# A linear-attention and spectral-mix kernel: where the channel products stand, and which engine takes the absorbs out of PSUM

## The chip, the cores and the metric

The kernel runs on one core of a Trainium2 chip. The metric is the device time of one execution in microseconds (us). Beside the times there is one profiled execution with its trace. The engines are called PE (matrix products), DVE (vector), ACT (scalar and activation), POOL (general, and here the queue that loads the weights) and SP (stores). In the stage of interest, PSUM is used as four buffers of one bank named `pt` and two buffers of two banks named `pp`.

## The reference

```python
def phi(x):                                   # q and k, per head, 576 x 64
    proj = x @ w_phi                          # 128 features
    proj = proj - max(abs(proj), axis=-1)
    return concat([exp(proj), exp(-proj)])
kv, z = phi(k).T @ v, phi(k).sum(axis=seq)
x = (phi(q) @ kv) / (phi(q) @ z + 1e-6)       # as (8, 576, 512)

X = rfft(x, axis=seq)                         # 64 of 289 modes are kept
Y[:, m] = X[:, m] @ (w_r[m] + 1j * w_i[m])    # 512 x 512 for each mode
u = x + irfft(Y, n=576)
out = u + relu(u @ w_ch)
```

Two of 8 batches make a batch pair `bp`. The weights `w_r`, `w_i` are 64 MB each in float32 and are all read once.

## The kernel before, in words

**Attention stage.** A loop of 19 steps over 16 units (channel group `g` of four, batch pair `bp` of four) fills `xs` (x in bfloat16, with positions in 9 chunks of 128 rows per batch pair) and `XT` (its kept modes). Weight tiles of 1 MB, one for each channel group, octet of modes `o` and part `i` (real, imaginary), arrive through POOL's queue in nine buffers `wt`, and each is used by a *mix*: eight matmuls `pt<-wt,XT` into one bank `py` per octet. Mixes for the first groups run inside the attention stage.

**The stage around the change.** The last 22 mixes come after it: what is left of the third channel group, octets 0 to 5 of the last one, then octet 6 and octet 7 with four mixes each (two groups, two parts). Each weight tile is waited for in that order. When an octet is complete, its result y goes from PSUM to `yst`, is transposed on PE to `yT`, is multiplied with `w_ch` into z (`zst`), and both are parked in `yacc` by DVE transposes (`park`). `lay(bp)` copies what is parked for one batch pair into `yall` and `zall`: two DVE transposes, and the same after octet 6 again for pair 0.

Between the mixes stands a list `todo` of small pieces, taken one by one by `fill(n)`; `n` is worked out from what is left of the list and of the mixes (`left`). It holds two kinds:

- *Channel products*, 36 chunks (`Channels`, lines 715 to 738). `turn` transposes a chunk of x on PE into a bank and copies it to `xT` by DVE; `product` multiplies it with `w_ch` into a bank, which ACT copies to `xw`. The first pieces also advance `inverse_tables`, which makes the tables CI, CL and CM, mostly on DVE, with three Sin activations on ACT.
- *Absorbs*, 36 chunks (`Absorb`, lines 750 to 802). `sum_p` makes the back transform of y for a chunk in p, and DVE adds it to x in place. `sum_q` does the same for z in q, with xw added by an identity matmul, and ACT copies q to xw. Of the first 28 absorbs in the list, every second is *aside*: it leaves out the identity matmul, ACT copies q to a spare tile `rl`, and POOL adds it to xw. Even places of the list take p and q as the two halves of one `pp` buffer, odd places as two `pt` buffers.

Before, three of the chunks (`ab[K:]`, K = 33) are treated apart: their products stay in PSUM (`hold` of `Channels`), and `only_x` and `only_w` finish them when `yall` and `zall` are there. The list is products 0 to 32, the three holds, three `only_x`, three `only_w`, 33 whole absorbs. Line 996 leaves two products for the place behind octet 5, and line 1001 spreads what remains over the last mixes:

```python
        if left > 8:
            n = -(-max(len(todo) - A - 2, 0) // (left - 8))
        elif left == 8:
            n = 2
        else:
            n = math.ceil(len(todo) / max(left - 0.6, 0.4)) if left else 0
```

The chunks that the tail needs first (`direct`, six of pair 0) are absorbed last, since they need octet 6 too. **The tail** begins with the last mix. Before it stand some identity matmuls ("bases"); behind it octet 7 is finished, and 18 pairs of chunks are summed, passed through relu and stored, in an order written out by hand (`plan`). All engines keep program order (`InOrder`); a wait of one instruction holds everything behind it on its engine.

Of the kernel before, what the change touches and what calls it, by code (L numbers as in the profile page):

```python
# [10 lines left out]
F32 = mybir.dt.float32  # L11
# [3 lines left out]
ALU = mybir.AluOpType  # L15
# [28 lines left out]
def kernel(  # L44
# [449 lines left out]
    def chunk(bp, n):  # L494
        if n < 8:
            return xs[:, :, bp, 2 * n:2 * n + 2, :].rearrange("p g h d -> p g (h d)")
        return xs[:, :, bp, 16:18, :].rearrange("p g h d -> p g (h d)")
# [100 lines left out]
    def bank(shape=(128, DMODEL), dt=F32):  # L598
        return pst.tile(list(shape), dt, name="pt", tag="pt")

    def banks(dt=F32):
        return pst2.tile([128, 2, DMODEL * (1 if dt == F32 else 2)], dt, name="pp", tag="pp")
# [112 lines left out]
    class Channels:  # L715
# [4 lines left out]
        def turn(self):  # L720
            x = chunk(self.bp, self.n)
            pt = bank([128, 4, 128], BF16)
            for g in range(NG):
                pe.transpose(pt[:, g, :], x[:, g, :], ident_b)
            self.xT = pb.tile([128, 4, 128], BF16, name="xT")
            dve.tensor_copy(self.xT, pt)

        def product(self):
            pf = bank()
# [2 lines left out]
                          start=(g == 0), stop=(g == 3))  # L732
            act.copy(xw[:, self.bp, self.n, :], pf)

        def hold(self, pf):
            for g in range(NG):
                pe.matmul(pf, lhsT=self.xT[:, g, :], rhs=wchb[:, g, :],
                          start=(g == 0), stop=False)

    def back(p, c, bp, table, src, r, stop=True, start=False):  # L740

        if c < 8:
            pe.matmul(p, lhsT=table[r, c % 4, :], rhs=src[r, 2 * bp + c // 4, :],
                      start=start or src is yall, stop=stop)
        else:
            for i in range(2):
                pe.matmul(p[64 * i:64 * i + 64, :], lhsT=table[r, 4, 0:64],
                          rhs=src[r, 2 * bp + i, :], start=start or src is yall, stop=stop)

    class Absorb:  # L750

        def __init__(self, bp, n):
            self.bp, self.n = bp, n
            self.early = (bp, n) in direct
            self.rows = slice(0, 128)
            self.aside = False

        def sum_p(self, p):
            self.p = p
            back(p, self.n, self.bp, CI, yall, self.rows)  # L760

        def sum_q(self, q):
            self.q = q
            if not self.aside:
                pe.matmul(q, lhsT=ident_b, rhs=xw[:, self.bp, self.n, :], start=True, stop=False)
            back(q, self.n, self.bp, CI, zall, self.rows, start=self.aside)

        def keep_x(self):
            x = chunk(self.bp, self.n)
            dve.tensor_tensor(out=x, in0=self.p.rearrange("p (g e) -> p g e", g=4),  # L770
                              in1=x, op=ALU.add)

        def keep_w(self):
            w = xw[:, self.bp, self.n, :]
            if self.aside:
                if not spare:
                    t = pb.tile([128, 2, DMODEL], F32, name="rl")
                    spare.extend((t[:, 1], t[:, 0]))
                t = spare.pop()
                act.copy(t, self.q)  # L780
                pool.tensor_tensor(out=w, in0=t, in1=w, op=ALU.add)
            else:
                act.copy(w, self.q)

        def only_x(self):
            self.sum_p(bank())
            self.keep_x()

        def only_w(self):
            back(self.q, self.n, self.bp, CI, zall, self.rows)  # L790
            self.keep_w()

        def all(self):
            if full.index(self) % 2:
                p, q = bank(), bank()
            else:
                t = banks()
                p, q = t[:, 0], t[:, 1]
            self.sum_p(p)
            self.sum_q(q)  # L800
            self.keep_x()
            self.keep_w()

    chunks = [(bp, n) for bp in range(NP) for n in range(9)]
    ch = [Channels(*c) for c in chunks]
    ab = [Absorb(*c) for c in chunks]
    K = len(ch) - 3
    full = sorted(ab[:K], key=lambda c: c.early)
    spare = []
    for c in full[0:28:2]:  # L810
        c.aside = True

    tables = inverse_tables()

    def hold(i):
        next(tables, None)
        if i + 1 < len(ch):
            ch[i + 1].turn()
        if i < K:
            ch[i].product()  # L820
            return
        if i == K:
            t = banks()
            ab[i].q, ab[i + 1].q = t[:, 0], t[:, 1]
        elif i == K + 2:
            ab[i].q = bank()
        ch[i].hold(ab[i].q)

    todo = [ch[0].turn] + [lambda i=i: hold(i) for i in range(len(ch))]
    todo += [c.only_x for c in ab[K:]] + [c.only_w for c in ab[K:]] + [c.all for c in full[:-2] + full[:-3:-1]]  # L830
    A = 3 * 3 + K

    def fill(n):
        for _ in range(n):
# [31 lines left out]
    class Pair:  # L866
# [32 lines left out]
        def sums(self, side, a):  # L899
            (bp, n), at, z = self.items[a], self.at(side, a), self.z(side)  # L900
            start = not self.based(side)
            if self.straight:
                pe.matmul(at, lhsT=CM[n // 4][:, n % 4], rhs=zst if z else yst, start=start,
                          stop=True)
            else:
                r = 64 * a + 32 * z
                back(at, n, bp, CL, yl, slice(r, r + 32), True, start)
            self.left[side] -= 1

        def keep(self, a):  # L910
# [63 lines left out]
        assert mark is None  # L974

    H = DMODEL // 2
    while mixq:
        key = mixq.pop(0)
        g, o, i = key[0], key[1] // 2, key[1] % 2
# [14 lines left out]
        if left == 6:  # L994
            yl = pw.tile([128, B_, DMODEL], BF16, name="yl", tag="wt")
        if left > 8:
            n = -(-max(len(todo) - A - 2, 0) // (left - 8))
        elif left == 8:
            n = 2
        else:  # L1000
            n = math.ceil(len(todo) / max(left - 0.6, 0.4)) if left else 0
        if g == NG - 1 and i == 1:
            end = left == 0
            py = pys.pop(o)
            yst = pb.tile([128, DMODEL], BF16, name="yst")
            pt = [bank([128, 2, 128], BF16) for h in range(2)]
            yT = [pb.tile([128, 2, 128], BF16, name=f"yT{h}") for h in range(2)]
            if end:
                dve.tensor_copy(yst[:, 0:H], py[:, 0:H])
                act.copy(yst[:, H:], py[:, H:])  # L1010
            else:
                for h in range(2):
                    dve.tensor_tensor(out=yst[:, H * h:H * h + H], in0=py[:, H * h:H * h + H],
                                      in1=(yacc[:, o] if o < 6 else late[:, o - 6])[:, H * h:H * h + H], op=ALU.add)
            put(yst, o, 0, (0, 2))
            if o < 5:
                fill(min(n, 1))
            for h in range(2):
                if end:
                    until(f"T{h}")  # L1020
                for dc in range(2):
                    pe.transpose(pt[h][:, dc, :],
                                 yst[:, H * h + 128 * dc:H * h + 128 * dc + 128], ident_b)
                if h or end:
                    dve.tensor_copy(yT[h], pt[h])
                else:
                    act.copy(yT[h], pt[h])
            if o < 7:
                park(yst, o, 0)
            if o < 5:  # L1030
                fill(min(n - 1, 1))
            cut = (slice(0, 384), slice(384, DMODEL))
            pz, marks = [], ["z0a", "z0b", "z1"]
            zst = pb.tile([128, DMODEL], BF16, name="zst")
            for e in range(2):
                for h in range(2):
                    if end and marks:
                        until(marks.pop(0))
                    if h == 0:
                        pz.append(bank([128, cut[e].stop - cut[e].start]))  # L1040
                    for dc in range(2):
                        pe.matmul(
                            pz[e], lhsT=yT[h][:, dc, :], rhs=wchb[:, 2 * h + dc, cut[e]],
                            start=(h == dc == 0), stop=(h == dc == 1))
                if e:
                    dve.tensor_copy(zst[:, cut[1]], pz[1])
                else:
                    act.copy(zst[:, cut[0]], pz[0])
            put(zst, o, 1, (1, 3))
            if o < 7:  # L1050
                park(zst, o, 1)
            if o == 5:
                lay(3)
                lay(0)
            elif o == 6:
                assert all(f.__self__.early or f.__self__.bp for f in todo)
                lay(0)
            fill(max(n - 2, 0) if o < 5 else n)
        else:
            fill(n)  # L1060
    assert not todo
# [33 lines left out]
```

## Time and profile before

| | |
|---|---|
| times of three runs | 436.51, 436.1, 438.81 us; median 436.51 |
| the profiled execution | 436.92 us |
| its span, first to last instruction | 435.1 us |
| mean granted PE clock | 0.911 of full speed |
| busy: PE, DVE, ACT, POOL | 75%, 70%, 67%, 28% of the span |
| octet 5's last mix | 356.29 us from the span's start |
| last weight tile issued | 365.83 us |
| last mix | 401.12 us |

How to read it: the page gives busy shares over the whole span, though stages have different limits; its slices are the span in 40 equal parts, one digit each for the busy tenths. A timeline row has start, length, engine, operation, result and operands, count, and the idle time before it with what ended it. All instructions carry one line number, that of the helper that records them, so tiles tell them apart: `xT`, `xw`, `xs`, `rl`, `wt`, `yall`, `zall`.

### The profile page before, as it was taken

To read this page: it belongs to the slowest core of one execution; us is meant where nothing else is said; L and a number is where in the kernel's file an instruction comes from. 1 tells how busy PE (TensorE), PEld (TensorE's weight loads), DVE (VectorE), ACT (ScalarE), POOL (GpSimd) and SP (SyncE) were. 2 spreads that over 40 slices of the span, in tenths; PEclk is the share of its full clock that TensorE was granted. 3 is DMA by queue.
4 is the path that set the end of the run, shared out by engine and by line. 5 is a ranking of instruction groups with operands and counts; after the bars stand their busy time and mean duration, and the time that the engine had idled before them with its cause. 6 is when DMAs were issued, how large, how long until landed. Compare 5 with 4: busy or idle time off the path is not lost.

```text
span 435.1 us, 10067 instructions
## 1 busy us (share of the span) xinstructions
PE 328.3 (75%) x4205; PEld 196.1 (45%) x4205; DVE 306.7 (70%) x608; ACT 291.5 (67%) x473; POOL 120.2 (28%) x158
## 2 busy tenths in 40 slices
PE   1567668678697686886976866946899867979993
PEld 1345546456465454554654644622345433333320
DVE  6768676765676677887678879728854445997794
ACT  3788696776977978887778779613444331656871
POOL 6232132123211212222222221221111100574790
PEclk9779897789988989997789999968999998999997
DMA  9999999999999999999999999999999999993797
GB/s 215 209 211 211 238 211 238 235 214 241 235 211 239 216 232 239 237 212 238 223 226 235 213 256 216 211 212 213 212 212 212 212 212 212 212 214 80 231 392 295
DMA packets 49879, 97.71 MB, mean 225 GB/s; under 512 B 2314, under 2 KB 11530, under 8 KB 49834
## 3 DMA queue, kind: packets, MB, share of 16 engines
q0 software_dynamic: 45136, 85.40, 100.4%
q1 hardware_dynamic: 4538, 11.60, 7.1%
q8 instruction: 33, 0.54, 0.5%
q10 hardware_dynamic: 160, 0.07, 0.1%
q14 instruction: 12, 0.10, 0.1%
HBM read 163.64 MB, written 9.44 MB: 398 GB/s over the span
## 4 chain that ended last, share of the span: by engine, by line
PE 34%; ACT 26%; DMA 17%; DVE 17%; issue 4%; POOL 1%; ACTq 0%; DVEq 0%; POOLq 0%
PE one L37 13%; ACT AQ L37 11%; ACT AB L37 9%; PE pt L37 8%; DMA wt<-in_moe_w_i_dram 8%; DMA wt<-in_moe_w_r_dram 8%; PE two L37 8%; DVE m L37 5%; PE pp L37 4%; ACT XT L37 3%; ACT qT L37 2%; DVE xs L37 2%; DVE mk L37 2%; DVE of L37 1%; DVE xw L37 1%
## 5 line engine op out<-in xcount | busy, mean ns | idle before, releaser
L37 ACT ACTIVATE AQ<-two 128x1024 bf16<-128x1024 f32 x64 | 80.4, 1345 | 2.0 <-PE two L37 1.9
L37 ACT ACTIVATE AB<-two 128x1024 bf16<-128x1024 f32 x64 | 62.8, 1054 | 3.3 <-DVE mk L37 3.1
L37 ACT CAST xw<-pt 128x512 bf16<-128x512 f32 x50 | 29.4, 588 | 44.8 <-PE pt L37 44.8
L37 DVE TENSOR_REDUCE m<-two 128x8 f32<-128x1024 f32 x32 | 39.2, 1224 | 20.1 <-PE two L37 20.0
L37 POOL DMA_DIRECT2D wt<-in_moe_w_i_dram x28 | 21.0, 750 | 88.3 <-PE one L37 33.2
L37 DVE TENSOR_REDUCE mk<-two 128x8 f32<-128x1024 f32 x32 | 38.9, 1217 | 8.8 <-PE two L37 8.8
L37 PE MATMUL pt<-wchb,xT 128*128 128x512 bf16 x136 | 38.1, 406 | 8.7 <-DVE xT L37 7.2
L37 PE MATMUL two<-w2blk,qT 128*128 128x256 bf16 x128 | 21.9, 299 | 27.0 <-ACT AQ L37 14.8
L37 DVE TENSOR_TENSOR va<-vn,ee 128x1152 bf16<-128x1152 f32 x32 | 41.9, 1354 | 0.0
L37 POOL DMA_DIRECT2D wt<-in_moe_w_r_dram x30 | 22.4, 746 | 66.4 <-PE one L37 20.3
L37 PEld LDWEIGHTS <-xs 128*128 128x128 bf16 x624 | 31.8, 103 | 13.1 <-issue 7.2
L37 ACT COPY qT<-one 128x512 bf16<-128x512 bf16 (+1 forms) x32 | 19.1, 642 | 24.7 <-PE one L37 24.5
L37 PE MATMUL two<-qT,w2blk 128*128 128x512 bf16 x64 | 27.1, 424 | 9.2 <-ACT AQ L37 9.2
L37 PEld LDWEIGHTS <-qT 128*128 128x128 bf16 x144 | 14.6, 103 | 41.8 <-issue 38.7
L37 DVE TENSOR_TENSOR xs<-one,rd 128x384 bf16<-128x384 f32 x48 | 26.7, 557 | 1.6
L37 PEld LDWEIGHTS <-AQ 128*128 128x128 bf16 x512 | 24.0, 106 | 7.7 <-issue 3.7
L37 PE MATMUL one<-kvz,AQ 128*128 128x65 bf16 x512 | 26.7, 206 | 0.9 <-ACT qT L37 0.8
L37 PE MATMUL two<-mT,minus 96*128 96x512 bf16 x64 | 27.3, 426 | 0.2 <-DVE mT L37 0.2
L37 PEld LDWEIGHTS <-XT 128*32 128x32 bf16 x512 | 14.6, 149 | 28.4 <-issue 21.1
L37 POOL DMA_DIRECT2D kb<-in_k_dram x16 | 11.4, 714 | 56.8 <-PE one L37 49.4
L37 PE MATMUL one<-wt,XT 128*32 128x512 bf16 x288 | 24.7, 430 | 2.9 <-ACT XT L37 1.5
L37 DVE RECIPROCAL rd<-one 128x6 f32<-128x6 f32 x48 | 9.4, 195 | 23.7 <-PE one L37 23.4
(150 smaller groups left out, 737.1 us busy)
## 6 DMA issues: line engine op xcount, KB each, us to landing
wt<-in_moe_w_r_dram POOLq DMA_DIRECT2D x30, 1024.0 KB, 27.7
wt<-in_moe_w_i_dram POOLq DMA_DIRECT2D x28, 1024.0 KB, 28.6
out_dram<-of SPq DMA_DIRECT2D x15, 512.0 KB, 3.9
vn<-in_v_dram POOLq DMA_DIRECT2D x13, 576.0 KB, 24.7
kb<-in_k_dram POOLq DMA_DIRECT2D x16, 288.0 KB, 19.9
qb<-in_q_dram POOLq DMA_DIRECT2D x16, 288.0 KB, 18.8
xs<-in_moe_w_i_dram POOLq DMA_DIRECT2D x2, 1024.0 KB, 23.2
out_dram<-of SPq DMA_DIRECT2D x6, 256.0 KB, 3.1
```

What stands on the lines that cost most here:

```text
L37: ins = f(*args, **kwargs)
```

## The change

All 36 products are made before the absorbs; the holds and their special pieces go. The first ten `xT` copies are made by ACT. Absorbs are sorted with batch pair 1 first, then 0, 2, 3, and the six direct chunks last. Of the first 32, places 0, 2, 4 and so on are aside (16), and places 1, 5, 9 and so on are *summed* (8): x itself is added into p by an identity matmul, and ACT copies p to x, where DVE added before. `fill(3)` runs before the first of the last mixes; three products are left for the place behind octet 5, and absorbs follow directly. Behind octet 5, pairs 1 and 0 are laid in place of 3 and 0; octet 6 takes pieces of the list between its own steps, as octets 0 to 4 do.

```diff
@@ Channels.turn
-            dve.tensor_copy(self.xT, pt)
+            if chunks.index((self.bp, self.n)) < 10:
+                act.copy(self.xT, pt)
+            else:
+                dve.tensor_copy(self.xT, pt)
@@ Absorb (sum_p, sum_q, keep_x, keep_w, only_x, only_w become one function)
+        def all(self):
+            if full.index(self) % 2:
+                p, q = bank(), bank()
+            else:
+                t = banks()
+                p, q = t[:, 0], t[:, 1]
+            x, w = chunk(self.bp, self.n), xw[:, self.bp, self.n, :]
+            rows = slice(0, 128)
+            pg = p.rearrange("p (g e) -> p g e", g=4)
+            if self.summed:
+                pe.matmul(pg, lhsT=ident_b, rhs=x, start=True, stop=False)
+            back(p, self.n, self.bp, CI, yall, rows, not self.summed)
             if not self.aside:
+                pe.matmul(q, lhsT=ident_b, rhs=w, start=True, stop=False)
+            back(q, self.n, self.bp, CI, zall, rows, self.aside)
+            if self.summed:
+                act.copy(x, pg)
+            else:
+                dve.tensor_tensor(out=x, in0=pg, in1=x, op=ALU.add)
             if self.aside:
...
+                act.copy(t, q)
                 pool.tensor_tensor(out=w, in0=t, in1=w, op=ALU.add)
             else:
+                act.copy(w, q)
@@
-    K = len(ch) - 3
-    full = sorted(ab[:K], key=lambda c: c.early)
+    full = sorted(ab, key=lambda c: (c.early, (1, 0, 2, 3)[c.bp]))
     spare = []
-    for c in full[0:28:2]:
-        c.aside = True
+    for i, c in enumerate(full[:32]):
+        c.aside, c.summed = i % 2 == 0, i % 4 == 1
@@ hold(i)
-        if i < K:
-            ch[i].product()
-            return
...
+        ch[i].product()
@@
-    todo += [c.only_x for c in ab[K:]] + [c.only_w for c in ab[K:]] + [c.all for c in full[:-2] + full[:-3:-1]]
-    A = 3 * 3 + K
+    todo += [c.all for c in full[:-2] + full[:-3:-1]]
+    A = len(full)
@@ the last mixes
+    fill(3)
     while mixq:
...
-            n = -(-max(len(todo) - A - 2, 0) // (left - 8))
+            n = -(-max(len(todo) - A - 3, 0) // (left - 8))
         elif left == 8:
-            n = 2
+            n = len(todo) - A
         else:
-            n = math.ceil(len(todo) / max(left - 0.6, 0.4)) if left else 0
+            n = math.ceil(len(todo) / max(left - 0.4, 0.6)) if left else 0
...
-            if o < 5:
+            if o < 5 or o == 6:
                 fill(min(n, 1))
...
-            if o < 5:
+            if o < 5 or o == 6:
                 fill(min(n - 1, 1))
...
             if o == 5:
-                lay(3)
+                lay(1)
                 lay(0)
...
-            fill(max(n - 2, 0) if o < 5 else n)
+            fill(max(n - 2, 0) if o < 5 or o == 6 else n)
```

## The prediction

> **What bounds the kernel now.** I read the utilisation slices first, then the chain that ended last, then the busy time in stretches cut at the mixes (the eight matmuls `pt<-wt,XT`), then the timeline of each engine.
>
> The slices show the DMA engines full until slice 35: the weights come in at about 212 GB/s, so one 1 MB weight tile every 4.95 us. The last one is issued at 365.83 and needs 30.2 us to land (the shortest landing of the tile `wt`), so it is there at 396.0. But the last mix starts only at 401.12. From octet 5 on, the kernel is therefore not waiting for weights but for the absorbs that stand between the mixes.
>
> ```profile
> PE   1567668678697686886976866946899867979993
> ...
> DVE  6768676765676677887678879728854445997794
> ...
> PEclk9779897789988989997789999968999998999997
> DMA  9999999999999999999999999999999999993797
> ```
>
> The stretches (columns: start and end, length, busy time and count of PE, weight loads, DVE, ACT, POOL, granted clock, DMA share, GB/s) run from octet 5's last mix (356.29) to the first whole absorb (371.71), to octet 6's last mix (380.27), to octet 7's first (388.71), to the end of the absorbs (399.31), to the last mix (401.12), to the end.
>
> ```profile
> 366.35:371.71 5.36, 4.71 (x31) 1.92 (x29) 3.22 (x6) 0.82 (x2) 0.22 (x1) 1.00 1.12 212
> 371.71:380.27 8.56, 8.08 (x45) 2.85 (x43) 7.83 (x14) 6.31 (x12) 5.74 (x5) 1.00 1.12 212
> 380.27:388.71 8.44, 6.10 (x40) 2.61 (x38) 7.59 (x16) 4.07 (x8) 5.00 (x8) 1.00 1.12 212
> 388.71:399.31 10.60, 10.60 (x66) 4.14 (x66) 9.30 (x16) 8.18 (x15) 7.57 (x7) 1.00 0.67 142
> ...
> 401.12:435.10 33.98, 25.52 (x153) 8.13 (x152) 23.10 (x25) 20.07 (x38) 18.62 (x17) 0.92 0.78 294
> ```
>
> PE is full in two of them; in the third, around octet 6, DVE is full and PE is not. The tail of 34.0 us starts with the last mix, and the change does not touch it. So the question is one number: when does the last mix start?
>
> **Prices, all from rows between 371 and 401 us.** A 512-column matmul takes 0.216 us of PE (371.71, 371.93, 372.15); a chunk 8 pair 0.24. A mix takes 0.68 with the gap before it. A DVE add takes 0.69 alone and 0.60 in a row; a lay is two transposes, 1.2. An ACT copy takes 0.59 alone, 0.49 in a row. A matmul's result is there 0.41 after its start.
>
> ```profile
> 372.35 0.69 DVE L37 TENSOR_TENSOR xs<-pp,xs 128x512 bf16<-128x512 f32 x1 [0.34 <-PE pp L37]
> ...
> 373.07 0.59 ACT L37 COPY rl<-pp 128x512 f32<-128x512 f32 x1 [0.53 <-DVE xs L37]
> 373.56 0.59 ACT L37 CAST xw<-pt 128x512 bf16<-128x512 f32 x1
> ```
>
> These three rows matter most: ACT's copy out of `pp` starts only when DVE's add out of the other half of that tile has ended (9 such waits, 6.5 us). Everything behind it in ACT's queue waits too.
>
> **The change, part by part.** (1) *Products.* By the counts that `n` gives, 31 of 36 were done before when octet 5's last mix came, then two more and three held in PSUM. Now 33 are done by then and three follow. That is two more in front (2 x 1.09 us, 352.13 to 353.22). PE waits 0.89, 0.5 and 2.05 us for weights at 346, 351 and 356 and 3.87 at 287.7 to 291.58, where `fill(3)` now stands. So they cost nothing; without that cover, 2.2. The ten xT copies on ACT take at most 0.64 each (row `qT<-one`), where ACT idles 8.65 us before its first product copy. Octet 5's mix stays at 356.29, set by its weights.
>
> (2) *Start of the absorbs.* DVE lays two batch pairs until 363.44, as before, and then copies xT twice; two products and the first mix of octet 6 follow: 363.89 + 2 x 0.86 + 0.74 = 366.35. Before, at 371.71, three of 36 absorbs' worth were done. So the change starts 5.36 us earlier with three absorbs more.
>
> (3) *Work.* 16 absorbs aside (2 matmuls), 8 with the added identity (4), 12 plain (3): 100 matmuls, 21.6 us of PE; with six mixes (4.1), octet 6's transposes and product (1.1), chunk 8's extra and its gaps (0.8) and the bases before the last mix (1.8) it is 29.4. From 366.35, PE alone would be through at 395.75. Before, the same count (85 matmuls, 18.4 + 4.1 + 1.1 + 0.4 + 1.8 = 25.8) took 29.41: 3.6 us of PE were lost.
>
> (4) *Waits that the change adds.* DVE loses eight adds (4.8 us); ACT gains eight copies, and they stand in the wrong place. ACT's order per four absorbs is rl, x, w, rl, w. The PSUM bank of a summed x is freed by ACT, and only after rl, which waits for DVE's add. With one of four `pt` banks held by the octet's accumulation, the plain absorb two places on needs that bank for its second half. First four absorbs, in us from 366.35: add 0.63 to 1.32, rl 1.34, x 1.83 to 2.42; PE is at the fourth absorb's second half at 1.95 and waits until 2.46. That is 0.5 each time where no mix or octet lies between. Up to octet 6's last mix this holds for absorbs 3 and 15 (counted from 0), and for 11 with 0.3: 1.3 us lost.
>
> (5) *Octet 6.* DVE's order is now y, lay(3), an add, then the copy of yT's second half; ACT has yT's first half behind rl, which waits for that add. Counted from its mix's start: y at 0.71, lay(3) at 1.47, add at 2.65, rl at 3.36, yT at 3.85, product at 4.28. Before, with nothing in between:
>
> ```profile
> 380.27 0.66 PE L37 MATMUL pt<-wt,XT 128*32 128x512 bf16 x8
> 381.78 0.62 PE L37 MATMUL pt<-ident_b,yst 128*128 128x128 bf16 x4 [0.85 <-DVE yst L37]
> 382.53 1.05 PE L37 MATMUL pt<-wchb,yT 128*128 128x384 bf16 x8
> ...
> 387.05 0.38 PE L37 MATMUL pp<-yall,CI 128*128 128x512 bf16 x1 [1.31 <-ACT rl L37]
> ```
>
> it stood at 2.26. PE has two absorbs and four transposes to cover 4.28, and loses 2.3. Then z, its park, lay(0), an add, rl and x come in turn before absorb 23 gets its bank (product to rl took 3.88 in these rows, 382.53 to 386.41, and x follows 0.49 later with 0.59 of its own): 1.2 lost. Together 3.5.
>
> (6) *Late.* Absorb 27 waits 0.5 as in (4); absorb 31's two halves share one bank, as the changed program is built, and the second waits for DVE: 1.3; absorb 34 waits 0.3. So 2.1.
>
> Sum of the losses: 1.3 + 3.5 + 2.1 = 6.9. POOL has two more adds (2 x 1.16), off this path. The last base waits 0.3 for the copies of absorb 35. 366.35 + 29.4 + 6.9 + 0.3 = 403.0: the last mix is 1.9 us later than before.
>
> What the trace does not show: ACT's copy with a strided result (x). Nearest rows: contiguous 0.59, and AQ against AB 1.345 to 1.054, 28% more for a stride in every element. Here 128 elements lie together, so I take 0.59; the other end is 0.75, eight times, 1.3 us. At the other end of (4) to (6), PE loses no more than before (3.6): 399.4.
>
> The profiled execution took 436.92 for a span of 435.1, so 438.8 by this sum; it lay 0.4 above the median of 436.51, and I take 438.4.
>
> **A rule on the clock.**
>
> ```profile
> 354.47:357.88 3.41, 1.02 (x12) 0.40 (x11) 0.76 (x2) 0.42 (x2) 0.00 (x0) 1.00 1.13 213
> 357.88:361.29 3.41, 3.30 (x17) 1.80 (x18) 1.78 (x5) 0.83 (x2) 0.00 (x0) 0.50 1.12 211
> 361.29:364.71 3.42, 1.63 (x11) 0.70 (x9) 2.87 (x6) 0.59 (x1) 0.00 (x0) 1.00 1.12 211
> ```
>
> A 3.41 us window with 1.02 of PE work is followed by one at half speed, one with 1.63 is not. The Trainium skill (TensorE: Matmul & The Clock Gate, Part 1: The HAM clock gate) says the clock halves after at least one idle window of about 3.4 us. By that rule octet 6's wait of 2 us would cost nothing more; these rows show that a partly idle window is enough. By the rule the sum stays 438.4; by the rows it may become the 440.0 of the third rival.
>
> **Rivals.**
> *The relief wins (faster).* DVE was full around octet 6 and loses 4.8 us of adds. If ACT takes x out as soon as it is there, (4) and (6) vanish and PE loses no more than the 3.6 of before: last mix at 399.4, 1.7 earlier than before, 434.8. It decides from a loss below 5.4. For it: ACT had room (4.07 of 8.44). Against it: ACT's 6.5 us behind DVE's adds, and its fixed order.
> *Weights set the end again.* No loss at all: PE at 395.75, weights at 396.0, mix at 396.1, 431.5, 1.1% faster. Against it: the chain in (5) is longer than its cover by rows alone.
> *Half clock in octet 6 (slower).* A window with 2.3 us of waiting is granted half speed. The product and three absorbs behind it (2.8 us of PE) double, of which 1.2 falls into the wait that follows: +1.6, 440.0; with the dear copy as well, 441.3. For it: the first row above. Against it: 379.20 to 382.60 had 1.97 of PE work and stayed at full speed.
>
> **How the numbers follow.** The forecast: 0.62, 438.4, by itself 437 to 440. The relief: 0.15. Weights: 0.04. Half clock or dear copies: 0.19. The range from 434.5 to 441.3 leaves out the second rival and what lies past the far end of the last. One per cent, about what a measurement of this kernel can tell, is 432.1 to 440.9. Below lies the second rival and a little of the first: 0.06. Above: nearly half of the last and the forecast's own edge, some 0.14. Between: 0.80.
>
> **What would show it.** In the profile after: first absorb's `pp<-yall,CI` at 366 to 367; ACT's x copies (`xs<-pt`) at 0.59, each behind an rl that waits for DVE; PE idle of 2 us before octet 6's `pt<-wchb,yT`, and over 1 us near 389; last mix near 403, and 34 us behind it. DVE less busy and ACT more, with PE idle between them. A last mix before 400 makes (4) to (6) wrong; a first absorb after 368 makes (2) wrong.

## The result, and the profile after

| | before | after |
|---|---|---|
| median of 19 runs each, us | 436.59 | 439.50 |
| profiled execution, its span | 436.92, 435.1 | 439.50, 437.7 |
| octet 5's last mix | 356.29 | 355.94 |
| first whole absorb | 371.71 (three of 36 already taken) | 366.72 |
| last mix | 401.12 | 404.11 |
| from the last mix to the end | 33.98 | 33.6 |

The ratio of after to before is 1.0056, 95% interval 1.0039 to 1.0073: 0.6% slower, inside the one per cent of "no change" and within the predicted range. The absorbs do begin 5 us earlier, and the last mix still comes 3 us later. The utilisation slices of after:

```profile
PE   2567658778688677787796787978987778978993
...
DVE  6778686657786777985778787777444354774794
...
PEclk9989898689898999996989997988999898999998
DMA  9999999999999999999999999999999999991697
```

In the 35th to the 37th slice (372 to 405 us) DVE's digits fell from 9, 9, 7 to 7, 7, 4, and PE's did not rise: 9, 7, 8 where they had been 9, 7, 9. The relief of DVE is there; PE got nothing from it. The DMA digit of the 37th slice is 1: the weights were all there while the last absorbs still ran.

The same stretches as before, cut at the first whole absorb (366.72), octet 6's last mix (380.98), octet 7's first (388.11), the end of the absorbs (402.02) and the last mix (404.11). Columns: start and end, length, busy time and count of PE, weight loads, DVE, ACT, POOL, then granted clock, DMA share, GB/s.

```profile
366.72:380.98 14.26, 13.24 (x76) 4.94 (x72) 9.62 (x15) 10.36 (x20) 9.64 (x9) 1.00 1.12 212
380.98:388.11 7.13, 5.34 (x36) 2.03 (x35) 5.53 (x12) 3.39 (x7) 4.75 (x7) 1.00 1.12 212
388.11:402.02 13.91, 11.10 (x65) 4.13 (x65) 8.06 (x13) 9.46 (x18) 6.99 (x7) 1.00 0.55 116
402.02:404.11 2.09, 1.98 (x8) 0.49 (x7) 0.69 (x1) 0.71 (x2) 0.00 (x0) 1.00 0.00 0
404.11:437.70 33.59, 25.93 (x153) 8.17 (x152) 23.17 (x25) 20.18 (x38) 18.60 (x17) 0.96 0.79 297
```

In none of the three long stretches is any engine full: PE misses 1.0, 1.8 and 2.8 us; ACT misses more in each, and DVE in the first and the third (in the second it misses 1.6). That is the picture of engines that wait for each other in an order, not of one that has too much work. The timeline of PE in after shows where it stopped (start, length, instruction, and in brackets the idle time before it and who ended it):

```profile
369.21 0.38 PE L37 MATMUL pt<-xw,ident_b 128*128 128x512 bf16 x1 [0.38 <-ACT xs L37]
...
375.37 0.38 PE L37 MATMUL pt<-xw,ident_b 128*128 128x512 bf16 x1 [0.21 <-ACT xs L37]
...
379.16 0.38 PE L37 MATMUL pt<-xw,ident_b 128*128 128x512 bf16 x1 [0.43 <-ACT xs L37]
...
385.18 1.05 PE L37 MATMUL pt<-wchb,yT 128*128 128x384 bf16 x8 [1.75 <-ACT yT L37]
...
390.18 0.38 PE L37 MATMUL pt<-xw,ident_b 128*128 128x512 bf16 x1 [1.08 <-ACT xs L37]
...
393.14 0.38 PE L37 MATMUL pt<-xw,ident_b 128*128 128x512 bf16 x1 [0.43 <-ACT xs L37]
...
397.99 0.38 PE L37 MATMUL pt<-xw,ident_b 128*128 128x512 bf16 x1 [1.17 <-DVE xs L37]
```

These seven waits are 5.45 us together, and every one of them is ended by ACT or DVE taking something out of PSUM. Counting the absorbs from 0, they stand at absorbs 3, 11 and 15, at octet 6's product, and at absorbs 23, 27 and 31. The timeline of ACT says why the x copy, the second row, is late: it has no wait of its own, but the row ahead of it has.

```profile
368.09 0.59 ACT L37 COPY rl<-pp 128x512 f32<-128x512 f32 x1 [1.58 <-DVE xs L37]
368.57 0.59 ACT L37 CAST xs<-pt 128x512 bf16<-128x512 f32 x1
```

In the waits of after, between 366.7 and 404, ACT's rl waits for DVE's xs 11 times, 9.9 us in all, up from 9 times and 6.5 us.

### The profile page after: what moved, and what is told of

The parts are those of the page before. It is cut to its first block, busy times and chain, and to the rows that moved or that the text cites. A ratio compares the mean times of both kernels' runs of the same rounds, so it can differ in the third digit from the quotient of the medians.

```text
span 437.7 us, 10101 instructions
## 1 busy us (share of the span) xinstructions
PE 332.0 (76%) x4214; PEld 196.7 (45%) x4214; DVE 299.6 (68%) x590; ACT 301.5 (69%) x494; POOL 122.4 (28%) x160
## 4 chain that ended last, share of the span: by engine, by line
PE 34%; ACT 24%; DMA 22%; DVE 14%; issue 4%; POOL 1%; DVEq 0%; ACTq 0%; POOLq 0%
DMA wt<-in_moe_w_i_dram 17%; PE one L37 12%; PE pt L37 11%; ACT AQ L37 10%; PE two L37 7%; ACT AB L37 6%; DMA kb<-in_k_dram 6%; DVE m L37 5%; PE pp L37 4%; ACT qT L37 3%; DVE xs L37 2%; ACT XT L37 2%; DVE mk L37 1%; DVE xw L37 1%; DVE small L37 1%
## 5 line engine op out<-in xcount | busy, mean ns | idle before, releaser
L37 ACT CAST xw<-pt 128x512 bf16<-128x512 f32 x54 | 32.0, 592 | 40.2 <-PE pt L37 40.1
L37 PE MATMUL pt<-wchb,xT 128*128 128x512 bf16 x144 | 41.4, 417 | 6.4 <-ACT xT L37 3.0
```

The costliest lines, as they stand in the source:

```text
L37: ins = f(*args, **kwargs)
```

## The experiments

The theory: the change costs time by ACT's order. An aside absorb's rl copy waits for DVE's add out of the same `pp` tile, and the x copy that the change gives to ACT stands behind it. The rivals: ACT now has too much to do; DVE's lay(3) ahead of octet 6's product; the split of octet 6; the early products. Twelve kernels were made from the changed one. The table gives, for each profiled execution, the first whole absorb, the last mix, the time between, and PE's busy time between; so a start that varies is told apart from a pace that does. Idle is the difference of the two. The ratio is to the kernel before.

| | first absorb | last mix | between | PE busy | idle | median, us | ratio, 95% interval |
|---|---|---|---|---|---|---|---|
| after | 366.72 | 404.11 | 37.39 | 31.66 | 5.73 | 439.50 | 1.0056 [1.0039, 1.0073] |
| 1 no identity | 365.80 | 399.27 | 33.47 | 29.94 | 3.53 | 435.54 | 0.9967 [0.9952, 0.9982] |
| 2 x first | 366.55 | 398.96 | 32.41 | 30.75 | 1.66 | 434.55 | 0.9941 [0.9922, 0.9959] |
| 3 lay(3) early | 366.37 | 402.97 | 36.60 | 31.51 | 5.09 | 438.84 | 1.0042 [1.0026, 1.0057] |
| 4 and octet 6 whole | 365.73 | 401.98 | 36.25 | 31.52 | 4.73 | 438.49 | 1.0033 [1.0019, 1.0047] |
| 5 = 2 + 3 | 366.21 | 397.94 | 31.73 | 31.11 | 0.62 | 434.31 | 0.9933 [0.9907, 0.9958] |
| 6 = 2 + 4 | 367.89 | 400.93 | 33.04 | 31.11 | 1.93 | 434.72 | 0.9937 [0.9919, 0.9955] |
| 7 tiles swapped | 366.85 | 400.22 | 33.37 | 31.29 | 2.08 | 435.59 | 0.9957 [0.9939, 0.9975] |
| 8 early part as before | 366.31 | 404.14 | 37.83 | 33.18 | 4.65 | 439.65 | 1.0052 [1.0030, 1.0075] |
| 9 late xT copies on ACT | 364.32 | 401.72 | 37.40 | 31.66 | 5.74 | 437.21 | 1.0003 [0.9984, 1.0023] |
| 10 = 5 + 9 | 365.06 | 396.77 | 31.71 | 31.10 | 0.61 | 432.31 | 0.9880 [0.9856, 0.9905] |
| 11 = 10, no identity | 363.52 | 396.50 | 32.98 | 30.06 | 2.92 | 432.48 | 0.9895 [0.9875, 0.9915] |
| 12 = 10 + 7 | 364.62 | 398.57 | 33.95 | 31.02 | 2.93 | 433.17 | 0.9909 [0.9887, 0.9932] |

The kernel before was measured beside each group of kernels. Its medians there were 436.94 (1 to 4), 437.82 (5 to 8) and 436.73 us (9 to 12), so kernels of different groups are best compared by their ratios. A profile shows one execution: the profiled executions of kernels 6 (436.33) and 12 (434.36) are 1.6 and 1.2 us above their medians, that of kernel 4 (437.37) is 1.1 below. Kernels 1 to 4 have three or four matmul records fewer in this stretch than their programs issue (175 and 176 of 179 in kernels 2 to 4), so their idle is a little too high.

**1. No absorb by the identity.** ACT's x copies and PE's identity matmuls are gone; everything else of the change stays.

```
-        c.aside, c.summed = i % 2 == 0, i % 4 == 1
+        c.aside = i % 2 == 0
```

> The changed kernel without the summed absorbs: DVE adds x in all 36. Theory (the summed x is taken out by ACT, but stands there behind an rl copy that itself waits for DVE, and its bank is then missing on PE): the 2.5 us in which PE waits for ACT's x copies go, and 8 identity matmuls (1.7 us) with them; DVE gets 4.8 us of adds back and PE loses about 3.6 to 4 us in all, as before the change. Last mix near 399, time 434 to 436, faster than before the change. Rival A (ACT has too much work, in whatever order): the same direction, at most 2.5 us less than now, 437. Rival B (DVE bounds this stretch, and the summed absorbs relieved it): slower than now, 441 or more.

Measured: 435.54, the last mix at 399.27. Without its relief of DVE the rest of the change is faster than before by 0.3%. So the part that was to help costs about 4 us, of which 1.7 is PE's own work (31.66 us busy with it, 29.94 without), and the earlier start is worth having. This leaves open whether the copies cost by their amount or by their place.

**2. The same copies, in another place.** The aside absorb keeps its rl copy, and POOL's add behind it, back until the next absorb's x or xw copy: behind the x copy of a summed absorb, in front of the xw copy of a plain one. `flush` issues what is kept in `behind`; its definition is left out here.

```
             if self.summed:
                 act.copy(x, pg)
+                flush()
...
-                act.copy(t, q)
-                pool.tensor_tensor(out=w, in0=t, in1=w, op=ALU.add)
+                behind.append((t, q, w))
             else:
+                flush()
                 act.copy(w, q)
```

> The changed kernel with one order changed on ACT and POOL: the copy rl of an aside absorb is issued behind the x copy of the next absorb, not ahead of it. No work is added or taken. Theory (order): the waits for x at absorbs 3, 11, 15, 27 (0.4 + 0.2 + 0.4 + 0.4) go, that at 23 shrinks from 1.1 to 0.3, octet 6's yT copy no longer stands behind an rl (0.8). Last mix 2 to 3.5 us earlier, time 436 to 437.5. Rival A (amount of ACT's work): nothing changes, 439.5.

Measured: 434.55, more of a gain than the theory expected and 5 us below the changed kernel, with the same work on every engine. ACT's timeline at the first absorbs of this kernel, to be read beside the two rows of after:

```profile
367.66 0.59 ACT L37 CAST xs<-pt 128x512 bf16<-128x512 f32 x1 [1.44 <-PE pt L37]
368.14 0.59 ACT L37 COPY rl<-pp 128x512 f32<-128x512 f32 x1
368.62 0.60 ACT L37 CAST xw<-pt 128x512 bf16<-128x512 f32 x1
369.21 0.59 ACT L37 COPY rl<-pp 128x512 f32<-128x512 f32 x1
```

The x copy now waits only for PE and starts 1.11 us behind the first absorb, where it was 1.85 in after; by the time rl is reached DVE's add is done, and the wait of 1.58 is no longer there. This decides between place and amount. PE's waits up to the last mix fall from 5.45 to 1.26 us (0.73 before octet 6's product and 0.53 for an rl copy). Of this fall, 1.17 is the wait at absorb 31, which the expectation had not counted. That this absorb gets another bank in the program as it is then built may be the reason; the views used here leave out buffer numbers and do not show it.

**3 and 4. Octet 6.** Kernel 3 issues lay(3) in front of octet 6's last mix, kernel 4 also takes the two absorbs out from between octet 6's parts.

```
+        if left == 5:
+            lay(3)
...
-            if o < 5 or o == 6:
+            if o < 5:
```

The first part is in both kernels; the second is one of three such places in kernel 4.

> The changed kernel with lay(3) five absorbs earlier, behind the third mix of octet 6, so that DVE has only one add between y and yT. Theory: octet 6's product starts 1.2 us earlier after its mix (3.0 in place of 4.2 us), what follows moves with it, and DVE's 1.2 us fall where it waits for PE anyway: time 438.3 to 438.8. Rival (that chain is covered by the two absorbs between): 439.5.

> As the run with lay(3) early, and octet 6's steps again without absorbs between them, as before the change. Theory: the product starts about 2.3 us after the mix as before the change, PE waits 1.2 to 1.5 us in place of 2.2, and z, its park and lay(0) come 0.8 us earlier than with lay(3) early alone: 437.5 to 438.3. Rival (the absorbs between hide more than they delay): slower than lay(3) early alone, 439 to 440.

Measured: 438.84 and 438.49, the first at the edge of what was expected, the second between what the theory and its rival gave. With lay(3) early the product came 3.02 us behind its mix (4.20 in after) and waited 0.56 for yT in place of 1.75, but the wait at absorb 15, in front of which lay(3) now stands, grew from 0.43 to 0.81; from first absorb to last mix it is 0.8 less. So lay(3) is a real cost, but a small part of the whole: while ACT's order stands, little is won at octet 6. Kernel 4 is 0.35 under kernel 3, both between first absorb and last mix and by the median, and the intervals of the two ratios overlap.

**5 and 6. Both repairs.**

> Both repairs together: an aside absorb's copy out of pp is issued behind the next absorb's x copy, and lay(3) stands before octet 6's last mix instead of between its y and its product. Same work. Theory (ACT's order is the loss, and lay(3) in DVE's queue is what still delays octet 6): octet 6's product, which stood 1.5 us later than it could in the version with the first repair alone, comes about 0.6 earlier; lay(3) itself now lies before the mix where DVE has room. Last mix 398.0 to 398.6, 433.8 to 434.3, that is 0.3 to 0.8 less than with x first alone. Rival (after the first repair PE is already full around octet 6, so the lay costs nothing): the same within 0.2, 434.4 to 434.7. Floor: the last weights land near 396.0, so no less than 431.5.

> As the one before, and octet 6's y, yT, product and z stand together, with no absorb between them, as in the kernel before the change. Theory: with the product 2.3 us behind its mix and nothing between, PE waits about 1.4 for yT but the absorbs behind find their banks free earlier: 433.8 to 434.8, no gain over the split version. Rival (the two absorbs between the parts cover nothing, their adds only delay yT): 0.5 to 1 better than the split version, 433 to 433.6.

In kernel 5 PE is busy 31.11 of 31.73 us: it is the bound again. That is 0.7 us less between first absorb and last mix than with x first alone; the medians, 434.31 and 434.55 from two chips, do not tell them apart. Kernel 6 is 1.3 us longer between than kernel 5 in the profiles: PE waits 0.54 for y and 0.81 for an rl copy behind octet 6, where kernel 5 waits 0.17. By the medians it is 0.4, and the intervals of the ratios do not tell the two apart. So the traces say that the two absorbs between octet 6's parts cover something once ACT is in order, and that without that (kernels 3 and 4) they did not; the times do not show it.

**7. The tile, not the engine.** One condition turned round: aside absorbs take two `pt` banks, the others the two halves of a `pp` tile. Instructions and their order on each engine are those of the changed kernel.

```
-            if full.index(self) % 2:
+            if full.index(self) % 2 == 0:
                 p, q = bank(), bank()
```

> The changed kernel with one condition turned round: aside absorbs take two separate pt banks, and the others (with the identity, or plain) take the two halves of a pp tile. Instructions, their order on each engine and the arithmetic are the same; only which PSUM tile a result lies in differs. Theory (ACT's rl copy waits for DVE's add because both read halves of one tile): rl no longer waits for DVE, the x copies behind it come at once, both copies of an absorb with the identity are ACT's own; only the plain absorbs' w (8 of them) now waits for DVE's add. 434.0 to 436.0, last mix 398.5 to 400.5, and the waits of ACT's rl for DVE's xs fall from 11 to 0 to 2, while those of ACT's xw for DVE's xs rise to 5 to 8. Rival (ACT's order or its amount of work is the loss, whatever the tile): 438.5 to 439.5. Rival B (a wait for a PSUM bank takes its place, since aside absorbs now draw on the three pt banks that the octets leave): 440 or more.

Measured: 435.59. The waits of after and of this kernel in their absorbs (total us, count, longest):

```profile
ACT rl L37 <- DVE xs L37: 9.9, 11, 2.5
...
ACT xw L37 <- DVE xs L37: 1.6, 2, 0.8
```

```profile
ACT xw L37 <- DVE xs L37: 7.0, 8, 2.2
```

The waits of rl for DVE are gone (no such row is left), and those of xw have risen from two to eight, most of them at plain absorbs (neither aside nor summed), which now have both results in one `pp` tile. So the wait goes with the tile: in these traces the copy out of one half of a `pp` tile starts only when the other engine's read of the other half has ended. That it costs 4 us less there is, by the order of the queues, again a matter of place: behind a plain absorb's xw comes an rl, which only POOL needs, and not the x copy. This reading was not tried by itself.

**8. The early part as before.** The first ten xT copies are DVE's again, and `fill(3)` is gone.

> The changed kernel with its early part as before: the ten first xT copies are DVE's again and fill(3) ahead of the mixes is gone; the absorbs are as changed. Theory (the early part lies under the weights): the same time, 439.0 to 440.0, octet 5's last mix within 0.3 of 355.94. Rival (the early products are what lets the absorbs start at 366.7): octet 5's last mix or the first absorb later by over 0.5, 440 to 442.

Measured: 439.65, and octet 5's last mix at 356.28, waiting for its weights. So `fill(3)` and the ten copies on ACT cost nothing and bring nothing by themselves. This execution showed one thing more, told below under the clock.

**9 to 12. The start.** In kernel 5 two products wait 1.62 us for xT copies that stand behind four lay transposes on DVE, while ACT idles. Kernel 9 is the changed kernel with the last three xT copies on ACT; 10 is kernel 5 with them; 11 is 10 without the identity absorbs; 12 is 10 with the tiles swapped.

```
-            if chunks.index((self.bp, self.n)) < 10:
+            if chunks.index((self.bp, self.n)) not in range(10, 33):
                 act.copy(self.xT, pt)
```

> The changed kernel with only that: the xT copies of the last three chunks on ACT. Theory (here ACT's order sets the pace behind the start, so an earlier start moves all absorbs by the same amount): first absorb 364.5 to 365.3, last mix 402.0 to 402.8, 437.4 to 438.4. Rival (the pace behind the start takes it up): 439 to 439.6.

> The version with x first and lay(3) early, and the xT copies of the last three chunks on ACT as well (ACT idles 1.8 and 2.3 us there; on DVE two of them stand behind four transposes of the lays, until 363.35). Theory (with the late waits gone, what is left is when the absorbs start): the last two products no longer wait 1.62 for DVE and run at full speed, the first absorb moves from 366.21 to 364.2 to 364.8, the mixes follow, and the last stands at the landing of its weights or just behind: 396.0 to 396.8, 432.0 to 433.2. Rival (other waits take the time back, as PE would be early for DVE's adds): last mix 397.5 to 398, 433.9 to 434.5.

> As the first of these, but with no absorb by the identity: DVE adds all 36 x. It tells what the relief of DVE is worth once ACT's order is mended. DVE has eight adds more, 4.8 us, in a stretch of some 32 us in which it was busy for about 24. Theory (ACT's order cost more than the relief gives, but the relief gives something): 433.3 to 434.8, 0.8 to 1.5 more than with it. Rival (DVE has room, the identity is only PE's extra 1.7 us): equal or faster by up to 1, 431.5 to 432.5.

> As the first of these, with the tiles swapped too (aside absorbs in two pt banks, the others in a pp tile). Theory (either repair takes rl's wait away, so the second adds nothing, and it makes the plain absorbs' w wait for DVE, and holds pt banks longer): 432.5 to 434.5, not faster than without the swap. Rival (what waits of rl for DVE are left in the first still cost): faster by 0.3 or more.

Kernel 9: the first absorb 2.4 us earlier, the time to the last mix 37.40 against 37.39: the pace is set by what follows, and every us of start is kept. Kernel 10 has the lowest median, 432.31, 1.2% under before. Kernel 11 went against the theory: it ends the same, 432.48. Its time between, 32.98, is 1.3 longer, but its first absorb came 1.5 earlier, and near the end it met the weights, as its timeline shows:

```profile
391.50 0.66 PE L37 MATMUL pt<-wt,XT 128*32 128x512 bf16 x8 [0.33 <-DMA wt<-in_moe_w_r_dram]
```

The last mix follows 5.0 us behind. The issues of the last weight tile tell the rest; the last number is the time from issue to landing in us, first in kernel 10 (issued at 365.44), then in kernel 11 (363.90):

```profile
wt<-in_moe_w_i_dram POOLq DMA_DIRECT2D x1, 1024.0 KB, 31.3
```

```profile
wt<-in_moe_w_i_dram POOLq DMA_DIRECT2D x1, 1024.0 KB, 32.6
```

The last weights landed at 396.7 and 396.5, and the last mixes started at 396.77 and 396.50. So in both kernels the last mix stands at the landing of its weights, and a better pace than kernel 10's could not have been seen in the time. What the identity absorbs are worth is therefore read from the pace alone. Kernel 11's stretch is 1.3 us longer, of which 0.33 is the wait for weights, so they are worth about 0.9 (PE idles 2.9 without and 0.6 with them, and is busy 1.0 longer with them). Kernel 12 shows that the second repair of the same wait brings nothing: PE then waits 0.94 and 0.73 us for rl copies to leave `pt` banks, and 1.08 for a late add of DVE. By the medians this costs 0.9, with ratio intervals that overlap.

## Why the prediction was right, and where it was not

**The forecast** put the last mix at 403.0 and it came at 404.11; the tail was 0.4 shorter. The time, 438.4, stood 1.1 under the median of 439.50.

**(1) Products:** free, as said. Octet 5's last mix came at 355.94 and still waited 1.18 for its weights; kernel 8 shows that the products are free without `fill(3)` and the copies on ACT, too.

**(2) Start:** 366.72 for 366.35, which is closer than its parts. The mechanism (DVE's lays, then two xT copies) held; kernel 9 shows it by taking the copies off DVE. But the copies began at 362.25, where the sum had 363.44:

```profile
362.25 0.71 DVE L37 COPY xT<-pt 128x512 bf16<-128x512 bf16 x2
362.69 3.19 PE L37 MATMUL pt<-wchb,xT 128*128 128x512 bf16 x8 [2.41 <-DVE xT L37]
```

So the two products began 1.20 early, at 362.69. They and the mix then took 4.03 us for the 2.46 of the sum, 1.57 more, since the clock was halved there, which the sum had not put in. In before the halved stretch lay in front of the lays, in this execution behind them; the last section tells why that differs. Of the two errors 0.37 is left, by luck:

```profile
359.75:363.17 3.42, 1.01 (x9) 0.48 (x8) 3.22 (x7) 0.58 (x1) 0.00 (x0) 0.99 1.13 213
363.17:366.58 3.41, 3.41 (x15) 0.92 (x13) 0.00 (x0) 1.17 (x2) 0.00 (x0) 0.50 1.12 212
```

**(3) Work:** the term that was mis-sized. PE was to need 29.4 us; where it is nearly full, in kernels 5 and 10, it is busy 31.1. The window of kernel 10 from first absorb to last mix:

```profile
365.06:396.77 31.71, 31.10 (x179) 11.69 (x176) 23.67 (x40) 23.91 (x47) 21.15 (x21) 1.00 1.06 207
```

The busy time of before would have told it. The prediction's count for before has six mixes behind 371.71, but the timeline has five (at 374.64, 380.27, 388.71, 393.01 and 397.41); with five it gives 25.1 us, and PE was busy 26.59 in those 29.41 us. That is the same 6% too low: 29.4 times 26.59/25.1 is 31.1. So before lost 2.8 us of PE and not 3.6. What the 6% consists of is not shown.

**(4) The order on ACT:** right, and the main cause, shown by kernel 2. The single waits were 0.38, 0.21 and 0.43 for the 0.5, 0.3 and 0.5 expected.

**(5) Octet 6:** the product stood 4.20 behind its mix for 4.28, and the wait at absorb 23 was 1.08 for 1.2. PE's wait before the product, though, was 1.75 for 2.3. Kernel 3 shows lay(3) as a part of it.

**(6) Late:** absorb 27 waited 0.43 (0.5), absorb 31 1.17 (1.3), absorb 34 nothing (0.3).

So losses of 7.2 (6.9 and the base's 0.3) stand against 5.7 of idle PE, and 29.4 of work against 31.7 busy. The two errors have opposite signs and leave 0.8 of 37.4. In part they are one error seen twice: octet 6's product came when the sum said, but PE's work in front of it was longer than counted, so the wait was shorter. That the rest nearly cancels is luck: the sum was better than its terms.

**The strided copy** took 0.59, as the value that was chosen; the far end of 0.75 fell away.

**The rivals.** *The relief wins* named its condition, ACT taking x out as soon as it is there, and its time, 434.8; kernel 2 nearly makes that condition true and gives 434.55, with the same two errors in the terms (PE idles 1.66 us, not 3.6). *Weights set the end* was wrong in its reason: with 31.1 us of work from 366.35 PE is through at 397.4, after the weights, so with that start it could not have come; kernels 10 and 11, with an earlier start, reach it. *Half clock in octet 6* did not come in after's profiled execution, but it did in kernel 8's (last section). Its price there was 1.6 us up to octet 7's first mix (8.72 between the mixes for 7.13), as said, but most of it was given back: the next mix came 4.42 behind for 5.56, since the wait of 1.08 at absorb 23 vanished. From first absorb to last mix kernel 8 took 37.83 for 37.39, so 0.44 of the 1.6 was left. The rival had counted a delay of PE in full where ACT's order set the pace.

## What to carry to other kernels

Before work is moved to an engine that idles, ask what it will stand behind in that engine's queue: here the place alone was worth 5 us. Behind an instruction that waits for another engine the eight copies, with their matmuls, cost about 4 us; in front of it the stage was 1.1 us shorter with them than without (kernels 2 and 1). Where two engines take out the two halves of one PSUM tile, look in the trace for the one waiting for the other, and at what stands behind that wait. To find what a change does to a stage, measure the stage from its first to its last event: the start and the pace then part, and a gain in either shows even where the end is held by something else.

## What the runs showed of the hardware that was not expected

**The half clock goes by windows that lie on one grid.** The prediction read from rows that a 3.41 us window with 1.02 of PE work is followed by half speed and one with 1.63 is not. Octet 6 in kernel 8 has one with 1.62 that is:

```profile
381.81:385.22 3.41, 1.62 (x10) 0.70 (x11) 3.25 (x7) 1.69 (x4) 2.40 (x4) 1.00 1.12 212
385.22:388.63 3.41, 3.41 (x15) 1.28 (x13) 2.22 (x5) 0.48 (x1) 1.51 (x3) 0.50 1.12 212
```

In octet 6, the changed kernel kept full speed. And behind octet 5's wait for weights, kernels 10 and 11 differ, though both have 1.23 us of PE work from 355.10 to 358.51. Kernel 10:

```profile
355.10:358.51 3.41, 1.23 (x12) 0.44 (x11) 0.85 (x3) 0.42 (x2) 0.00 (x0) 1.00 1.12 212
358.51:361.93 3.42, 3.37 (x15) 1.90 (x16) 2.05 (x5) 1.06 (x3) 0.00 (x0) 0.50 1.12 211
```

It cost kernel 10 1.65 us there (5.91 from octet 5's product to the next mix, 4.26 in kernel 11), which accounts for its start, 1.54 later. The reason is where the windows are cut. Within each profile, every change of the clock falls on one grid from start to end; in before, the changes at 286.20 and 357.88 are 21 steps of 3.413 us apart. From one execution to the next the grid shifts: its first edge lies 2.89, 1.32 and 0.13 us behind the start of the span in before, after and kernel 10. In kernel 11 the clock changed at 304.73, so its windows meet 14, 15 and 16 steps later, at 352.51, 355.93 and 359.34, and not at 355.10. Its two windows there hold 2.12 and 1.92 us of work, and the one of octet 6 in the changed kernel (third row) holds 1.85:

```profile
352.51:355.93 3.42, 2.12 (x16) 1.05 (x13) 0.42 (x1) 1.66 (x3) 0.40 (x1) 1.00 1.12 212
355.93:359.34 3.41, 1.92 (x17) 0.86 (x17) 1.58 (x4) 0.37 (x1) 0.00 (x0) 1.00 1.13 213
...
383.61:387.03 3.42, 1.85 (x14) 0.96 (x15) 2.53 (x7) 1.83 (x4) 1.72 (x3) 1.00 1.12 211
```

Cut on their own grids, the 14 profiles have 1401 windows at full clock. All 166 with up to 1.54 us of PE's busy time are followed by half speed, none of the 1122 with 1.93 or more, and 28 of the 113 between. What decides between 1.55 and 1.92 us stays open. So whether a wait of PE halves the clock depends on where the grid cuts it, and that differs from run to run. The Trainium skill (TensorE: Matmul & The Clock Gate, Part 1: The HAM clock gate) says that the window runs free of the kernel and that half speed follows at least one idle window. The first agrees with these traces. The second does not agree with these rows, where the windows in front of half speed hold 1.23 and 1.62 us of PE work.

**ACT's copies out of PSUM all cost the same here.** At 128 by 512 they took about 0.59 us into f32, into bfloat16, contiguous or in runs of 128, and in a row they start 0.48 apart.
